# Third batch's q and k transposed by the DMA queue instead of TensorE: a threshold moved from 3 to 2

## The chip, the cores and the metric

The kernel runs on one core of one Trainium2 chip. The metric is device microseconds (us) of one launch, lower is better. Before the change three runs took 271.57, 271.71 and 272.1 us, a median of 271.71 us.

## The reference: what is computed

Inputs are q, k and v of shape (8 batches, 8 heads, 576 rows, 64 columns) and two weight matrices, w_in (512 x 2048) and w_out (2048 x 512), all float32. The output is 4608 x 512 float32. For each batch and head, a Nyström attention with 32 landmarks, and then one feed-forward layer over all heads' columns together:

```python
q_lm = q.reshape(B, H, m, S // m, D).mean(axis=3)     # m = 32 landmarks
k_lm = k.reshape(B, H, m, S // m, D).mean(axis=3)
A  = sm(q, k_lm)                                      # softmax of scaled scores
Bm = sm(q_lm, k_lm)
C  = sm(q_lm, k)
Z = Bm.T / (norm1(Bm) * norminf(Bm) + 1e-6)
for _ in range(6):
    Z = 2 * Z - Z @ Bm @ Z                            # inverse by Newton steps
x = A @ Z @ C @ v                                     # heads side by side: 4608 x 512
out = relu(x @ w_in) ** 2 @ w_out
```

## The kernel before, in words

**Stages.** The eight batches are numbered 0 to 7 here, so the "third batch" is batch 2. The kernel is a pipeline of stages, one for each batch b. In stage b, TensorE does the first product of the feed-forward layer for batch b (`mlp_in`, line 656: 16 pieces f of four matmuls), carries on with the second product for earlier batches (`mlp_out`, line 686), and between these does the attention of batch b+1. The attention is a Python generator, `attention(b + 1, R)`, that yields after each small piece. The main loop (lines 721 to 765) decides after which f how many pieces of it are issued: `steps` pieces in all (line 729), six tenths of them spread over the 16 pieces f, the rest over `mlp_out`. TensorE, VectorE and ScalarE then run in the order in which this weaving has put their instructions.

**The path of q and k.** For batch b, `load_qk` starts four transfers on GpSimd's DMA queue, which also convert float32 to bfloat16: the rows 512 to 575 of k and q into one small tile `qkt` (line 84), and the other 512 rows into `raw` tiles (line 96), two buffers shared by k and q. `prepare` copies a `raw` tile to `nat` on VectorE (line 188), which puts a head pair's columns side by side. The attention needs q and k both as they are (for the segment means, lines 253 and 263) and transposed, 128 x 128 block by block, as `T` (16 blocks each for q and k) and `tT` (four blocks from `qkt`). The transposed tiles are the stationary operands of the score matmuls (`scores`, line 408, and `tails`, line 418).

**Two ways to transpose.** Batches below `DMA_T` transpose on TensorE (lines 226 and 236) into PSUM, and VectorE or ScalarE copy the result to SBUF (lines 239, 548, 555, 558, 560). Batches from `DMA_T` on have it done by the DMA engines, issued from SP's queue: `tT` from line 196, `T` of k and of q from line 190, as soon as their source is there:

```python
            nc.vector.tensor_copy(X[nm][:], raw)
            if b >= DMA_T:
                nc.sync.dma_start_transpose(
                    X[nm + "T"].rearrange("p c a t -> p (c a) t"),
                    X[nm].rearrange("p c h d -> p (c h d)"))
```

**When `nat` is made.** The copies of line 188 are pinned behind a named instruction of the batch before (`kpin`, `qpin`). For batch 2 they are late: behind the copy to `WT` (line 609) and the last copy to `G` (line 642) of batch 1's attention, that is at the end of stage 0. For batch 3 and later they come behind the first joint step of the inverse of the batch before, which is in the middle of the stage ahead of the one that uses them.

**Weaving.** The same threshold sets `steps`: 28 where the attention in the stage transposes on TensorE, 24 where it does not. Of these 16 or 14 belong to the 16 pieces f. Within the attention the order is: segment means of k and of q, landmark scores and softmax, start of the inverse (lines 335 to 361), TensorE's transposes if any, and then pairs of an inverse step and a piece from `side`: scores of q (two halves), tails, scores of k (two halves), row sums, C times v.

**Queues.** GpSimd's DMA queue carries all loads from batch 1 on and both weight matrices, in program order; SP's queue carries batch 0's q and k, the DMA transposes and one of the last stores; ScalarE's queue carries the other stores.

Of the kernel before, what the change touches and what calls it, by code (L numbers as in the profile page):

```python
# [27 lines left out]
TAIL = S - NC4 * P  # L28
HALF = S // 2
SCALE = 1.0 / 8.0  # L30
DMA_T = 3


@with_exitstack
def kernel(
# [139 lines left out]
    def prepare(b: int, nms=("k", "q"), halves=((0, H),)):  # L175

        X = loaded[b]
        for nm in nms:
# [9 lines left out]
# [5 lines that stand above are left out]
        if "k" in nms:  # L193
            X["tT"] = attn.tile([P, NPAIR, P], BF16, tag="tT", name="tT")
            if b >= DMA_T:
                nc.sync.dma_start_transpose(X["tT"][:], X["qkt"].rearrange("p h d -> p (h d)"))
# [13 lines left out]
    def attention(b: int, R: dict):  # L210
# [6 lines left out]
        def transposed(nm, half):  # L217
            if not first:
                tps = ntile([P, 2, NPAIR, P], BF16)[:]
            else:  # L220
                if half == 0:
                    X["tps"] = psum.tile([P, 4, NPAIR, P], BF16, tag="h", bufs=2, name="tps")
                tps = X["tps"][:, 2 * half:2 * half + 2, :, :]
            for i in range(2):
                for p in range(NPAIR):
                    nc.tensor.transpose(
                        tps[:, i, p, :],
                        X[nm][:, 2 * half + i, 2 * p:2 * p + 2, :].rearrange("p h d -> p (h d)"),
                        ident_bf[:],
                    )  # L230
            return X[nm + "T"][:, 2 * half:2 * half + 2, :, :], tps
# [303 lines left out]
        else:  # L535
# [10 lines left out]
            yield  # L546
            if b < DMA_T:
                dve(*transposed("q", 0))
# [4 lines left out]
            yield  # L553
            if b < DMA_T:
                act(*transposed("q", 1))
# [165 lines left out]
    for b in range(B):  # L721
# [6 lines left out]
        att = attention(b + 1, R) if b + 1 < B else iter(())  # L728
        steps = 28 if b + 1 < DMA_T else 24
        half = steps * 6 // 10  # L730
# [67 lines left out]
```

The softmax here doesn't subtract the row's maximum and nothing guards it: scores larger than these inputs give would overflow.

## Time and profile before

One execution was profiled. Its own time was 271.57 us, with a span of 269.9 us from the first to the last instruction.

| what | value |
|---|---|
| median of three runs | 271.71 us |
| profiled execution: time, span | 271.57 us, 269.9 us |
| TensorE matmuls busy | 249.3 us (92% of the span) |
| VectorE busy, ScalarE busy | 176.2 us, 159.3 us |
| first `mlp_in` matmul of stages 1, 2, 3, 4 | 54.51, 84.71, 116.09, 144.37 us |
| DMA of loads (GpSimd's queue) | 17.17 MB |
| DMA of SP's queue (batch 0's q and k, transposes) | 8.39 MB |

Times are microseconds from the start of the span. An engine's busy time counts its data instructions; a matmul's end is modelled, since matmuls overlap. In a timeline, a row gives start, length, engine, line, operation, output and inputs, their shape, and how many instructions were merged; in brackets stands how long the engine stood idle before it, and what ended that. A name ending in q (SPq) is the engine's instruction queue, where DMAs are issued; the length of such a row is the time that issuing took, not that of the transfer. "DMA to landing" runs from the issue to the last byte's arrival.

### The profile page before, as it was taken

The page shows a single profiled execution, that of the slowest core. Times are in us where ns is not written, and L with a number is a line of the kernel's source. Part 1 is how long each engine was busy: PE and PEld are TensorE (multiplying, and loading weights), DVE is VectorE, ACT ScalarE, POOL GpSimd, SP SyncE. Part 2 cuts the span into 40 slices and gives each one's busy share as a digit, 9 for nine tenths or more (in the row PEclk, how much of TensorE's full clock was granted, in tenths as well). Part 3 has the DMA queues.
Part 4 walks back from the last instruction along what each step waited for, and adds up shares of the span by engine and source line. Part 5 has one row for each costly group of instructions (what it writes and reads, how often), then busy time and mean ns, then how long its engine had stood idle before and what let it go on. Part 6 is the DMA issues. An engine that isn't in the chain of part 4 may idle for free.

```text
span 269.9 us, 6741 instructions
## 1 busy us (share of the span) xinstructions
PE 249.3 (92%) x2747; PEld 149.6 (55%) x2793; DVE 176.2 (65%) x493; ACT 159.3 (59%) x280; POOL 43.4 (16%) x66
## 2 busy tenths in 40 slices
PE   2988799979999999999999999999999999999994
PEld 0754565457654665456555665466545665466444
DVE  4687878668884769458955779459954768545100
ACT  2478866448926766468726774568636674487111
POOL 3834333310320230220220231100000000000000
PEclk9999999999999999999999999999999999999999
DMA  7999999999699959993999969991911111200222
GB/s 206 244 205 196 205 204 187 229 188 134 82 157 196 167 119 152 179 155 53 141 166 149 143 121 154 144 163 39 198 41 39 41 39 41 78 34 9 78 78 80
DMA packets 69791, 35.31 MB, mean 131 GB/s; under 512 B 37376, under 2 KB 64256, under 8 KB 69760
## 3 DMA queue, kind: packets, MB, share of 16 engines
q0 software_dynamic: 37696, 17.17, 54.7%
q1 hardware_dynamic: 26816, 8.39, 21.8%
q10 hardware_dynamic: 5248, 9.31, 10.8%
q8 instruction: 22, 0.36, 0.6%
q14 instruction: 9, 0.07, 0.1%
HBM read 36.70 MB, written 9.44 MB: 171 GB/s over the span
## 4 chain that ended last, share of the span: by engine, by line
PE 62%; DMA 18%; ACT 7%; DVE 6%; issue 4%; POOL 1%; ACTq 0%; DVEq 0%; POOLq 0%
PE ops L686 31%; PE h L656 15%; DMA w_out_bf<-in_moe_w_out_dram 6%; PE n L686 6%; DMA raw<-in_q_dram 5%; DMA w_in_bf<-in_moe_w_in_dram 5%; ACT r L663 3%; ACT G L640 2%; PE g L627 2%; DMA raw<-in_k_dram 2%; DVE ra L432 2%; DVE gT L664 2%; PE n L454 1%; PE n L253 1%; PE n L408 1%
## 5 line engine op out<-in xcount | busy, mean ns | idle before, releaser
L686 PE MATMUL ops<-w_out_bf,gT 128*128 128x512 bf16 (+1 forms) x451 | 114.5, 371 | 3.2 <-DMA w_out_bf<-in_moe_w_out_dram 1.0
L663 ACT ACTIVATE r<-h 128x576 bf16<-128x576 f32 x128 | 82.9, 658 | 29.3 <-PE h L656 24.6
L656 PE MATMUL h<-AT,G 128*128 128x288 bf16 x512 | 83.3, 285 | 2.7 <-ACT G L640 1.0
L664 DVE TENSOR_TENSOR gT<-r 128x576 bf16<-128x576 bf16 x128 | 58.0, 454 | 32.7 <-ACT r L663 31.6
L686 PEld LDWEIGHTS <-gT 128*128 128x128 bf16 x592 | 53.4, 97 | 39.9 <-issue 6.9
L656 PEld LDWEIGHTS <-G 128*128 128x128 bf16 x512 | 45.4, 97 | 22.2 <-issue 5.7
L695 ACT COPY o_sb<-ops 128x512 f32<-128x512 f32 (+1 forms) x29 | 16.7, 578 | 35.2 <-PE ops L686 35.2
L686 PE MATMUL n<-w_out_bf,gT 128*128 128x512 bf16 x98 | 28.7, 380 | 0.4 <-issue 0.2
L642 DVE CAST G<-g 128x1024 bf16<-128x1024 f32 x14 | 17.1, 1224 | 12.7 <-PE g L627 12.7
L640 ACT CAST G<-g 128x1024 bf16<-128x1024 f32 x14 | 14.2, 1012 | 11.2 <-PE g L627 11.2
L408 PEld LDWEIGHTS <-T 128*128 128x128 bf16 x256 | 11.3, 98 | 5.4 <-issue 0.4
L325 PEld LDWEIGHTS <-ED 128*128 128x128 bf16 x84 | 7.2, 98 | 11.4 <-DVE ED L316 5.3
L444 DVE TENSOR_TENSOR an<-EA,rra 128x640 bf16<-128x640 f32 (+2 forms) x17 | 13.2, 779 | 0.2
L432 DVE TENSOR_REDUCE ra<-EA 128x20 f32<-128x640 f32 (+1 forms) x19 | 13.0, 701 | 0.4
L408 PE MATMUL n<-bd,T 128*128 128x64 bf16 x256 | 12.8, 193 | 0.1
L458 ACT COPY AT<-n 128x576 bf16<-128x576 bf16 x9 | 5.8, 639 | 11.8 <-PE n L454 11.8
L106 POOL DMA_DIRECT2D vm<-in_v_dram x8 | 7.0, 881 | 34.4 <-PE n L476 23.6
L253 PEld LDWEIGHTS <-nat 128*128 128x128 bf16 x256 | 9.0, 97 | 5.9 <-DVE nat L188 2.6
L96 POOL DMA_DIRECT2D raw<-in_k_dram x7 | 7.1, 1018 | 29.5 <-DVE nat L188 27.1
L84 POOL DMA_DIRECT2D qkt<-in_k_dram x7 | 5.1, 730 | 41.5 <-PE n L263 28.6
L188 DVE COPY nat<-raw 128x2048 bf16<-128x2048 bf16 x14 | 9.4, 688 | 2.5 <-DMA raw<-in_q_dram 1.8
L412 ACT ACTIVATE EA<-n 128x512 f32<-128x512 f32 x16 | 9.5, 601 | 2.0 <-PE n L408 2.0
(125 smaller groups left out, 267.1 us busy)
## 6 DMA issues: line engine op xcount, KB each, us to landing
out_dram<-o_sb ACTq DMA_DIRECT2D x31, 256.0 KB, 4.4
vm<-in_v_dram POOLq DMA_DIRECT2D x8, 512.0 KB, 14.0
raw<-in_k_dram POOLq DMA_DIRECT2D x7, 512.0 KB, 9.6
raw<-in_q_dram POOLq DMA_DIRECT2D x7, 512.0 KB, 13.5
w_in_bf<-in_moe_w_in_dram POOLq DMA_DIRECT2D x4, 512.0 KB, 10.6
w_out_bf<-in_moe_w_out_dram POOLq DMA_DIRECT2D x4, 512.0 KB, 16.2
out_dram<-o_sb ACTq DMA_DIRECT2D x9, 128.0 KB, 2.4
raw<-in_k_dram SPq DMA_DIRECT2D x1, 1024.0 KB, 5.6
```

The lines of the kernel that those rows point to most:

```text
L253: nc.tensor.matmul(means[:, ti, p, :], lhsT=src.rearrange("p h d -> p (h d)"), rhs=seg[:, c + (ti if c == NC4 else 0), :], start=(n == 0 a ...
L408: nc.tensor.matmul(sc[:, c, j, :, :], lhsT=X[nm + "T"][:, c, p, :], rhs=BD[:, 1 if nm == "q" else 0, p, 0:64], start=True, stop=True)
L412: nc.scalar.activation((EA if nm == "q" else EC)[:, qd, 0:NC4, :], sc.rearrange("p c j i m -> p c (j i m)"), AF.Exp, scale=SCALE)
L432: nc.vector.reduce_sum(ra[:, quads, lo:hi, :], EA[:, quads, lo:hi, :].rearrange("p q c (h m) -> p q c h m", m=M), axis=AX.X)
L444: nc.vector.tensor_tensor(an[:, i, lo:hi, :].rearrange("p c (h m) -> p c h m", m=M), EA[:, i, lo:hi, :].rearrange("p c (h m) -> p c h m", ...
L640: nc.scalar.copy(dst, gg[:])
L642: last = nc.vector.tensor_copy(dst, gg[:])
L656: last = nc.tensor.matmul(h[:, j, 0:HALF], lhsT=G[:, qd, f * P:(f + 1) * P], rhs=AT[:, qd, j * HALF:(j + 1) * HALF], start=(qd == 0), stop ...
L663: nc.scalar.activation(r.rearrange("p (j t) -> p j t", j=2), h[:, :, 0:HALF], AF.Relu)
L664: return nc.vector.tensor_tensor(gT[:, f, o:o + S], r[:], r[:], ALU.mult)
L686: mark[:] = [nc.tensor.matmul(ops, lhsT=gT[:, f, t * P:t * P + P], rhs=w_out_bf[:, f, i * n:i * n + n], start=(f == 0), stop=(f == NF - 1))]
L695: nc.scalar.copy(o_h, ops)
```

## The change

One constant:

```diff
-DMA_T = 3
+DMA_T = 2
```

It is read in five places: in `prepare` (lines 189 and 195), where batch 2 now gets the three DMA transposes on SP's queue; in `attention` (lines 547 and 554), where batch 2's TensorE transposes and their copies go away; and in the main loop (line 729), where stage 1, which holds batch 2's attention, goes from 28 steps to 24:

```python
            if b < DMA_T:
                dve(*transposed("q", 0))
            yield
            begun = inverse_begin()
            yield
            BT, ED = inverse_first(*begun)
            yield
            if b < DMA_T:
                act(*transposed("q", 1))
                ...
                transposed_tail()
```

Put together, the order of instructions on the queues changes as follows.

- SP's queue, from its sixth instruction on, held `tT` of batch 3, `T` of k and of q of batch 3, `tT` of batch 4 and so on. It now holds `tT` of batch 2, `tT` of batch 3, `T` of k and q of batch 2, `T` of k and q of batch 3, `tT` of batch 4 and so on.
- TensorE loses 36 transposes in stage 1. The score matmuls of batch 2's q, which stood behind f = 10, now stand behind f = 7, and their weight load waits for the DMA transpose of q.
- VectorE loses three copies and ScalarE two. Elsewhere in stage 1 their instructions change places in keeping with the steps.
- GpSimd's queue is the same.

## The prediction

> **What bounds the kernel now.** I read the page first: engine busy times, and the DMA row of the 40 slices (6.75 us each).
>
> ```profile
> PE 249.3 (92%) x2747; PEld 149.6 (55%) x2793; DVE 176.2 (65%) x493; ACT 159.3 (59%) x280; POOL 43.4 (16%) x66
> ...
> DMA  7999999999699959993999969991911111200222
> ```
>
> TensorE sets the pace, so time that it stands still is time lost. But the DMA engines are full for the first ten slices, up to about 67 us: loads run behind. So I read the timeline around the end of stage 0, where batch 2's q arrives:
>
> ```profile
> 51.81 0.69 DVE L188 COPY nat<-raw 128x2048 bf16<-128x2048 bf16 x1 [0.79 <-DMA raw<-in_k_dram]
> 55.40 0.69 DVE L188 COPY nat<-raw 128x2048 bf16<-128x2048 bf16 x1 [1.76 <-DMA raw<-in_q_dram]
> 56.43 1.29 SPq L196 DMA_TRANSPOSE tT<-qkt  x1
> 57.28 0.65 PE L656 MATMUL h<-AT,G 128*128 128x288 bf16 x4 [0.79 <-DVE G L642]
> 67.37 0.40 PE L408 MATMUL n<-bd,T 128*128 128x64 bf16 x8
> 70.39 11.90 SPq L190 DMA_TRANSPOSE T<-nat  x2
> 187.74 4.62 SPq L190 DMA_TRANSPOSE T<-nat  x2
> ```
>
> Batch 2's q is in `nat` only at 56.1 us; its first scores (line 408) run at 67.37 us, 11.3 us later, with TensorE's transposes between. SP's row at 56.43 is batch 3's `tT`, whose wait had ended on the load of `qkt` (the queue's wait list gives 51.3 us on it). 70.39 is batch 3's pair of `T`, 187.74 the last batch's.
>
> Then the transposing DMAs' own times (line 190, by window; lengths and landings as min/median/max, which for two is k's, the mean, q's): batch 3's pair, batch 4's, and batch 7's, when no load is left:
>
> ```profile
> L190 SPq DMA_TRANSPOSE T<-nat x2: 2023/5892/9762, 70.4 to 72.5; - x2
> DMA to landing us min/median/max: 11.2/15.8/20.3
> ...
> L190 SPq DMA_TRANSPOSE T<-nat x2: 3018/5123/7228, 97.6 to 100.7; - x2
> DMA to landing us min/median/max: 9.6/11.5/13.5
> ...
> L190 SPq DMA_TRANSPOSE T<-nat x2: 1741/2266/2791, 187.7 to 189.6; - x2
> DMA to landing us min/median/max: 4.4/6.0/7.7
> ```
>
> From k's issue to q's landing a pair takes 189.6 + 7.7 - 187.7 = 9.6 us with the engines free, 100.7 + 13.5 - 97.6 = 16.6 us and 72.5 + 20.3 - 70.4 = 22.4 us beside loads.
>
> **What the Trainium skill says.** *DMA: Bandwidth & Descriptors*, "Queues, rings and completion order": each DMA engine goes round between its queues packet by packet. The trace agrees: between 56 and 66 us the load queue moved 1.42 MB while batch 3's `tT`, 0.13 MB, took 7.2 us to land. The same page, "Latency and other measured facts", has 261 GB/s for a transposing DMA; here the free pair moved 1.05 MB in 9.6 us, 109 GB/s, and I use that. *TensorE: Matmul & The Clock Gate*, "Step-by-step: what each phase is for": matmuls stay in program order, only weight loads are pulled ahead; the 0.79 us wait at 57.28 us, with other batches' matmuls queued behind it, fits. The same page, "What's actually happening": after an idle window of about 3.4 us TensorE's clock halves, until some 3.4 us of work. The trace shows the like at the start, after 4.15 us of idling (granted clock 1.00 all the same): three 128x512 matmuls took 1.34 us at 9.78 us, and three of that shape take 0.82 us at 115.10 us.
>
> ```profile
> 7.13 1.89 PE L226 MATMUL tps<-ident_bf,nat 128*128 128x128 bf16 x16 [4.15 <-DVE nat L185]
> 9.78 1.34 PE L202 MATMUL idle<-bd 128*128 128x512 bf16 x3
> 115.10 0.82 PE L686 MATMUL n<-w_out_bf,gT 128*128 128x512 bf16 x3
> ```
>
> **The change part by part.**
>
> *Removed.* 32 transposes of line 226 and 4 of line 236. A group of eight spans 0.61 us, the last lasting 0.22, so one costs (0.61 - 0.22) / 7 = 0.056 us, and 36 cost 2.0 us of TensorE. With them go two ScalarE copies (1.01 and 1.05 us) and three on VectorE (0.69, 0.69, 0.42). TensorE was busy for 10.00 us of 57.3 to 67.4, so up to 2.0 us is a real gain, if nothing else stops it.
>
> *Added, SP's queue.* `tT` of batch 2 comes first. Its `qkt` is issued at 31.20 us and lands some 11 to 16 us later, so it runs in the full stretch: 0.13 MB at the 165 GB/s or so that the engines move beside transposes is 0.8 us, which every load behind it, and so q's arrival, loses. Next is `tT` of batch 3, which waits for its own `qkt` (56.43 us, now about 57.2) and takes 1.29 us to issue. Both `T` of batch 2 stand behind it: although k is in `nat` at 52.5 us, its transpose goes out at about 58.5 us, and q's after that. GpSimd's load of batch 4's `qkt`, which waited for TensorE's transposes (line 236) until 66.9 us, waits now for `tT` and the means of line 263, both done by about 59 us: 0.13 MB more beside the transposes.
>
> *How long the pair takes.* In the before trace the load queue still moves about 1.1 MB after 57.8 us (batch 3's q and k). Add 0.13 MB `qkt`, 1.18 MB transposes (pair and the `tT` ahead of it) and one store of 0.26 MB: 2.65 MB at 165 GB/s is 16 us. That is close to batch 4's 16.6 us. So q's transpose lands at 58.5 + 16 = 74.5 us. Bounds: 57.7 + 9.6 = 67.3 us with engines free and no shift; 58.5 + 22.4 = 80.9 us at batch 3's pace.
>
> *When it is wanted.* With 14 steps in place of 16 in the f pieces, and no transposes ahead, the scores of q stand behind f = 7. Before, f = 7 begins at 63.43 us with two groups of eight transposes ahead of it (60.10 and 62.99 us); without them, and with f = 7 itself (0.65 us) done, the new order reaches the scores at about 63 us. Their weight load waits for q's DMA. Behind it on TensorE stands everything: f = 8 to 15, the second product, the inverse. ScalarE and VectorE run dry within a microsecond or two and wait too. The stall is 74.5 - 63 = 11.5 us.
>
> *From there on.* Stage 3 is the model: also 24 steps, DMA transposes, the same five second-product tiles at its end. It runs from 116.09 to 144.37, with its first scores at 124.16 us, so 20.2 us pass from the scores to the next stage. Stage 2 therefore begins at 74.5 + 20.2 = 94.7 instead of 84.71 us: 10.0 us late, the removed work already counted in. Were q in time, it would begin at 63 + 0.8 + 20.2 = 84.0, 0.7 us earlier than now. The break-even landing is 84.7 - 20.2 = 64.5 us.
>
> *Cold clock.* An idle TensorE of over 3.4 us should come back at half clock for about 3.4 us, losing up to 1.7; ScalarE's relu (0.65 us a piece) hides a little. I take 1.5; bounds 0 and 3.4 (two windows).
>
> *Later stages.* Batch 3's pair goes out 3.9 us after the scores in stage 3's pattern (128.03 against 124.16), so at 78.4; at 22.4 us it lands at 100.8, and is wanted 9.5 us into stage 2, at about 104 or later. No second stall; the rest shifts unchanged.
>
> Sum against the profiled execution: 271.57 + 10.0 + 1.5 = 283.1 us. This execution lies 0.14 us below the median, nothing in these terms; I say 283.
>
> **Rivals.**
>
> *The pair runs almost free* (landing at 67.3 to 70.5): the transposes take the better share of the engines. For it: batch 4's k moved at 171 GB/s when the loads had not begun. Against: here the load queue is in full flow. 271.6 + 2.8 to 6, and a cold start of 0 to 1.5: 274.5 to 279, middle 277.
>
> *The pair starves* (landing after 78): batch 3's pair took 22.4 us with one load pair beside it. 271.6 + 13.5 to 16.4 + 1.5 = 286.5 to 289.5, middle 288.
>
> *The transfer is hidden* (faster): q's transpose lands by 64.5 us, TensorE never waits, and the removed 2.0 us show as far as the delayed loads let them: 271.6 - 0.7 = 270.9 us. It decides at a landing of 64.5 us. That needs the pair in about 7 us from 57.7, against 9.6 at best; only an SP order that lets k out at 52.5 could do it, and the instruction order says otherwise.
>
> *The change is empty in effect*, a stall that just eats the gain, takes the same 64.5 us landing within half a microsecond.
>
> **How the numbers follow.** Late by 71 to 78: 0.72; almost free: 0.15; starved: 0.08; hidden 0.03; even 0.02. The forecast is the likeliest, 283. The range, 276 to 288, corresponds to landings from about 68 (with the cold start) to 79, and leaves out the hidden and even cases and the outer part of the two others, under 2 in 10. A measurement here tells about 0.2% (0.5 us) from no change: faster 0.03, same 0.02, slower 0.95.
>
> **What will show it.** TensorE idle once, before the score matmuls of line 408 near 63 us, for 7 to 15 us, ended by the DMA of `T` from `nat`; on SP `tT` twice, the second near 57 us, and then four `T`; q's landing near 74.5; longer matmuls for some 3 us after; stage 2's first `mlp_in` at 95 to 96 us; later stages as long as before. I am wrong if q's transpose lands before 65 us, if TensorE has other matmuls to do in the wait, or if the stages after it win the time back.

## The result, and the profile after

| | before | after |
|---|---|---|
| median, us | 271.83 (4 runs, the three given above and 271.95) | 282.01 (4 runs, 281.0 to 283.71) |
| ratio after / before | | 1.0381, 95% interval 1.0329 to 1.0433 |
| profiled execution: time, span | 271.57, 269.9 | 282.07, 280.3 |

The change makes the kernel 10.2 us slower. The page of the kernel after, its engine and slice rows (7.0 us a slice):

```profile
PE 250.3 (89%) x2711; PEld 148.8 (53%) x2757; DVE 174.7 (62%) x490; ACT 157.7 (56%) x278; POOL 43.1 (15%) x66
...
PE   2888999872499999999999999999999999999995
...
PEclk9997999997599999999999999999999999999999
DMA  7999999999569994996199989991541010101222
```

TensorE's busy time went up by 1.0 us although it has 36 matmuls fewer, and its share fell from 92% to 89%: the work is there, there is a hole in it. The hole is in slices 9 and 10 (counted from 0), 63 to 77 us, and the granted clock is down in the same two. (The 7 in slice 3 is another, short dip of this execution, from 22.7 to 26.1 us, where the kernel is the same as before.)

The timeline around it, rows of VectorE, SP's queue and TensorE that answer to those shown of before:

```profile
53.40 0.69 DVE L188 COPY nat<-raw 128x2048 bf16<-128x2048 bf16 x1 [1.51 <-DMA raw<-in_k_dram]
56.95 0.70 DVE L188 COPY nat<-raw 128x2048 bf16<-128x2048 bf16 x1 [1.72 <-DMA raw<-in_q_dram]
...
46.11 13.24 SPq L196 DMA_TRANSPOSE tT<-qkt  x2
59.47 28.67 SPq L190 DMA_TRANSPOSE T<-nat  x4
...
64.28 0.65 PE L656 MATMUL h<-AT,G 128*128 128x288 bf16 x4
73.99 0.61 PE L408 MATMUL n<-bd,T 128*128 128x64 bf16 x8 [9.06 <-DMA T<-nat]
95.38 0.65 PE L656 MATMUL h<-AT,G 128*128 128x288 bf16 x4 [0.17 <-ACT G L640]
```

TensorE ends f = 7 at 64.9 us and then does nothing until q's transpose lands; the first matmul of stage 2 follows at 95.38 us, 10.7 us later than before. From there to the end pass 184.9 us, before 185.2: nothing is lost or won later. The transposes themselves (line 190 between 55 and 76 us; the second view is of the first of the pair alone):

```profile
L190 SPq DMA_TRANSPOSE T<-nat x2: 6114/6182/6251, 59.5 to 65.7; - x2
DMA to landing us min/median/max: 8.3/10.6/12.9
...
T<-nat SPq DMA_TRANSPOSE x1, 12.9
```

k's goes out at 59.47 and lands at 72.4; q's goes out at 65.69 and lands 8.3 us later, at 74.0. Last, the windows of TensorE, from the start of stage 1 to behind the hole (stretch, its length, TensorE's busy time and matmuls, granted clock, DMA share, GB/s; the DMA share adds up the times of packets, and passes 1 where packets of several queues are open at once):

```profile
57.00:65.00 8.00, 6.17 (x61) 1.00 1.48 190
65.00:74.00 9.00, 0.01 (x1) 0.62 1.30 173
74.00:77.40 3.40, 3.40 (x21) 0.51 0.02 5
77.40:84.00 6.60, 6.38 (x64) 1.00 0.72 110
```

While TensorE waits, the DMA engines are full; when it starts again, they are empty. For its first 3.3 us its clock is half, and from then on full again.

### The profile page after: what moved, and what is told of

Same layout as the page of the kernel before. It is cut to its first block, busy times and chain, and to the rows that moved or that the text cites. A ratio compares the mean times of both kernels' runs of the same rounds, so it can differ in the third digit from the quotient of the medians.

```text
span 280.3 us, 6675 instructions
## 1 busy us (share of the span) xinstructions
PE 250.3 (89%) x2711; PEld 148.8 (53%) x2757; DVE 174.7 (62%) x490; ACT 157.7 (56%) x278; POOL 43.1 (15%) x66
## 3 DMA queue, kind: packets, MB, share of 16 engines
q10 hardware_dynamic: 5248, 9.31, 10.2%
## 4 chain that ended last, share of the span: by engine, by line
PE 62%; DVE 11%; DMA 10%; ACT 10%; issue 5%; DVEq 0%; ACTq 0%
PE ops L686 29%; PE h L656 14%; DMA raw<-in_q_dram 5%; ACT r L663 5%; PE n L686 5%; DVE gT L664 3%; DMA T<-nat 3%; PE g L627 2%; ACT G L640 2%; DMA raw<-in_k_dram 2%; PE n L253 2%; DVE ra L432 2%; PE n L454 2%; PE n L325 1%; PE n L408 1%
## 5 line engine op out<-in xcount | busy, mean ns | idle before, releaser
L686 PEld LDWEIGHTS <-gT 128*128 128x128 bf16 x592 | 53.5, 98 | 40.6 <-issue 7.5
L640 ACT CAST G<-g 128x1024 bf16<-128x1024 f32 x14 | 14.2, 1012 | 11.1 <-PE g L627 11.1
L408 PEld LDWEIGHTS <-T 128*128 128x128 bf16 x256 | 11.6, 99 | 14.5 <-DMA T<-nat 9.4
L330 DVE SCALAR_TENSOR_TENSOR EY<-EY,n 128x128 bf16<-128x128 bf16 x24 | 6.8, 283 | 12.7 <-PE n L325 12.6
L325 PEld LDWEIGHTS <-ED 128*128 128x128 bf16 x84 | 7.4, 99 | 11.5 <-DVE ED L316 4.9
L627 PE MATMUL g<-w_in_bf,WT 64*32 64x512 bf16 x232 | 9.6, 389 | 2.0 <-DVE G L642 1.0
```

The lines of the kernel that those rows point to most:

```text
L325: nc.tensor.matmul(res[a:a + w, qd, :], lhsT=diagonal[a:a + w, qd, :], rhs=moving(qd)[a:a + w], start=True, stop=True)
L408: nc.tensor.matmul(sc[:, c, j, :, :], lhsT=X[nm + "T"][:, c, p, :], rhs=BD[:, 1 if nm == "q" else 0, p, 0:64], start=True, stop=True)
L627: nc.tensor.matmul(g[i][M * p:M * p + M, :], lhsT=WT[64 * i:64 * i + 64, i, M * p:M * p + M], rhs=w_in_bf[64 * i:64 * i + 64, p, n * 512:n ...
L640: nc.scalar.copy(dst, gg[:])
L686: mark[:] = [nc.tensor.matmul(ops, lhsT=gT[:, f, t * P:t * P + P], rhs=w_out_bf[:, f, i * n:i * n + n], start=(f == 0), stop=(f == NF - 1))]
```

## The experiments

Line numbers of an experiment's kernel can stand a few lines below those quoted so far (line 408, the score matmuls, is L409 or L414 in some).

**Nobody transposes batch 2.** Is the wait all that the change costs?

```diff
-                X[nm + "T"] = attn.tile([P, NC4, NPAIR, P], BF16, tag=nm + "T", name="T")
+                X[nm + "T"] = (loaded[1][nm + "T"] if b == 2 else attn.tile(...))
...
-            if b >= DMA_T:
+            if b > 2:
                 nc.sync.dma_start_transpose(
```

(and the same for `tT`)

> The changed kernel, but batch 2 is transposed by nobody: its scores read batch 1's transposed tiles, so batch 2's output is not the reference's. TensorE's instructions are those of the changed kernel in the same order. Theory (the late landing of q's transpose is the whole loss): no wait ahead of the score matmuls of line 408 in stage 1, and the 2.0 us of TensorE transposes are gained in part: 269.8 to 271.3 us, below the 271.8 of the kernel before. Rival (the new order of stage 1, 24 steps for 28, costs time by itself): 272.5 us or more, with idle time in stage 1 that is not ended by a DMA.

Measured: 270.62 us, ratio 0.9954 (0.9937 to 0.9971). TensorE's timeline:

```profile
63.49 0.40 PE L409 MATMUL n<-bd,T 128*128 128x64 bf16 x8
...
83.90 0.65 PE L657 MATMUL h<-AT,G 128*128 128x288 bf16 x4 [0.16 <-ACT G L641]
```

The scores run at 63.49 us, without a wait ahead of them, and stage 2 begins 0.8 us earlier than in the kernel before. So the new order and the missing transposes together win 1.2 us (0.8 to 1.7), of the 2.0 us that the 36 transposes take; what the order with 24 steps is worth by itself was not tried. Against this run the kernel after loses 11.4 us by the medians, and the profiles account for it: its scores come 10.5 us later (73.99 against 63.49), and from them to stage 2 pass 21.4 us, not 20.4.

**q's transpose ahead of k's.** Does TensorE wait for q's transpose or for the pair?

```diff
...
+            if b == 2 and nm == "q":
+                one = turn("q")
+                with tc.issue_after(one.ins):
+                    X["lastT"] = turn("k")
+            elif b > 2:
+                turn(nm)
```

> The changed kernel with batch 2's two big DMA transposes in the other order: q's first, k's behind it. Theory (TensorE waits for q's landing alone): q's goes out when k's did, at about 59.5 us, and lands 8.3 us later as k's did, at about 68; TensorE waits some 3 us in place of 9.1. k's lands at about 74, and its scores come some 7 us after q's, so they wait little or not at all. 275 to 277 us. Rival (the pair's whole time on the DMA engines decides, whichever is first): the wait moves to the scores of k, and the time stays at 280 to 282 us.

Measured: 279.94 us, ratio 1.0283 (1.0243 to 1.0322). SP's queue (two `tT` and four `T` in this window), the landing of the first transpose, now q's, and TensorE:

```profile
58.65 26.77 SPq L190 DMA_TRANSPOSE T<-nat  x4
...
T<-nat SPq DMA_TRANSPOSE x1, 12.7
...
71.44 0.61 PE L414 MATMUL n<-bd,T 128*128 128x64 bf16 x8 [7.34 <-DMA T<-nat]
```

Both expectations missed the time. The theory's 8.3 us for the first transpose was a misreading: in the changed kernel that is the landing of the second, and the first takes 12.9. q first takes 12.7 us; the wait falls from 9.1 to 7.3 us only, the time by 2.1 us, and k's scores don't wait, against the rival. Which is first matters little, because in either order both land when the loads are nearly through (at 72.4 and 74.0 us in the kernel after, 71.4 and 73.0 here).

**Dummy matmuls in the hole.** What does the clock cost?

```diff
+        if b == 2:
+            filler = ntile([P, 512])
...
+            with tc.issue_after(front[0].ins):
+                for _ in range(36):
+                    mm = nc.tensor.matmul(filler[:], lhsT=z[:, 0:P], rhs=z[:, 0:512], ...)
+            with tc.issue_after(mm.ins):
+                aside()
```

> The changed kernel with 36 dummy matmuls of 128x512 (some 7.8 us) on TensorE in the place where it stands still, ahead of batch 2's first scores. Theory (TensorE comes out of the wait at half clock and loses 1.2 us by it: 21.4 us from the scores to the next stage, against 20.2 in stage 3): the granted clock stays at 1.00 and the time is 280.8 us, 1.2 below the changed kernel. Rival (the clock after the wait costs nothing, the 1.2 us have another cause): 282 us, and still 21.4 us from the scores to the next stage.

Measured: 280.52 us, ratio 1.0305 (1.0268 to 1.0342). TensorE's timeline:

```profile
64.34 7.93 PE L578 MATMUL n<-bd 128*128 128x512 bf16 x36
73.84 0.41 PE L408 MATMUL n<-bd,T 128*128 128x64 bf16 x8 [1.57 <-DMA T<-nat]
93.64 0.65 PE L666 MATMUL h<-AT,G 128*128 128x288 bf16 x4 [0.17 <-ACT G L650]
```

The transpose lands at the same time (73.84 against 73.99 us), the granted clock is 1.000 over the whole run (0.976 in the changed kernel), and from the scores to stage 2 pass 19.8 us instead of 21.4. The medians of the two kernels lie 1.5 us apart; each was timed beside its own runs of the kernel before (271.86 and 271.83 us). The intervals of the two ratios just overlap, so the 21.4 and 19.8 us of the profiles carry the point as much as the medians. Work that computes nothing makes the kernel faster. Two pieces f behind the scores also stand in another order here, so of the 1.5 us a few tenths may belong to that.

**Batch 3's loads taken away.** Are the transposes slow because of what moves beside them?

```diff
-            for lo, hi in parts:
+            for lo, hi in ((0, 1),) if b == 3 else parts:
...
```

> The changed kernel with batch 3's loads of q and k cut to one head in eight (the head is spread to all eight places, so batch 3's output is not the reference's): some 0.9 MB less stands beside batch 2's DMA transposes. Theory (the transposes are slow because they share the engines with the loads that run behind): the pair takes about the 9.6 us that the last batch's takes, q's lands at about 69 us, TensorE waits some 4 us, 276 to 277.5 us. Rival (the transposes are held up by their own issue on SP's queue, k's then q's, whatever else moves): q's still goes out about 6 us after k's and lands at 73 to 74; 281 to 282 us.

Measured: 277.09 us, ratio 1.0170 (1.0126 to 1.0213). The two `T` of batch 2 and TensorE:

```profile
L191 SPq DMA_TRANSPOSE T<-nat x2: 2990/3036/3082, 58.5 to 61.6; - x2
DMA to landing us min/median/max: 5.4/5.8/6.1
...
67.78 0.61 PE L409 MATMUL n<-bd,T 128*128 128x64 bf16 x8 [3.05 <-DMA T<-nat]
```

The pair goes out 1.0 us earlier than in the kernel after, is issued twice as fast (3.0 us each, not 6.2), and takes 61.6 + 6.1 - 58.5 = 9.2 us, not 14.5. This is the theory's case. Even so the kernel is slower than before: with most of the loads gone the transposes still come 3 us late. The profile is of the quickest of four runs (275.73 us, clock 0.994); the other three took 277.0 to 277.4 at 0.980. Their longer time at half clock fits that; they have no profile.

**Batch 3's small transpose behind.** Is it the place on SP's queue?

```diff
...
+                with tc.issue_after(loaded[2]["lastT"].ins) if b == 3 else nullcontext():
                     nc.sync.dma_start_transpose(X["tT"][:], ...)
```

> The changed kernel with batch 3's small DMA transpose put behind both big ones of batch 2 on SP's queue, in place of ahead of them; k's then goes out as soon as k is copied, at about 54, not 59.5 us. Theory (the engines' share decides: the transposes move only as the load queue lets them): they start moving some 4 us earlier, but the same bytes stand in front, and q, copied at about 57 us, is second; q's lands at 70 to 72 us, 279 to 281 us. Rival (the wait behind the small transpose on SP's queue is what makes them late): q's lands 5 us earlier, at 68 to 69 us, 275 to 277 us.

Measured: 282.64 us, ratio 1.0401 (1.0379 to 1.0424). SP's queue, the first transpose's landing, TensorE:

```profile
53.52 13.58 SPq L190 DMA_TRANSPOSE T<-nat  x2
...
T<-nat SPq DMA_TRANSPOSE x1, 12.9
...
73.64 0.61 PE L409 MATMUL n<-bd,T 128*128 128x64 bf16 x8 [9.54 <-DMA T<-nat]
```

k's goes out 6 us earlier and lands 6 us earlier, at 66.4 us. q's goes out 7.2 us earlier (58.5, not 65.7) and lands at 73.6 us all the same. So the queue in front of the transposes held k's, but not q's, the last of the pair. Moving earlier, they take from the loads: batch 3's k and q land 12.6 and 13.9 us after their issue, not 9.3 and 10.0. The theory had the kind right, but its 70 to 72 us for the landing, and its time with it, were too low.

**Batch 2's v behind its q and k**, on the kernel after (expected first below) and on the kernel before (second). Is it the late q?

```diff
...
-            load_v(b + 2, loaded[b + 2])
+            with tc.issue_after(loaded[2]["lastraw"].ins) if b == 0 else nullcontext():
+                load_v(b + 2, loaded[b + 2])
```

> The changed kernel with the same move: batch 2's v loaded behind its q and k. Theory (a transpose beside the full load queue gets a third of the engines, so that q's lands only when the loads have drained, whenever it was issued; the move leaves the bytes as they are): q and k are copied some 3 us earlier, their transposes still land at 71 to 74 us, TensorE reaches the scores earlier and waits longer, 280 to 282 us. Rival (it is the late arrival of q that makes its transpose late): q's lands 3 us earlier, at about 70 to 71 us, and the time falls by 3 to 278.5 us or below.

> The kernel before, with batch 2's loads of v (0.6 MB) put behind its q and k on GpSimd's queue, in place of ahead of them; nothing else changes place. Theory (the loads that run behind are the root: batch 2's q arrives late for TensorE even in the kernel before): q lands some 3 us earlier, at 52 to 53 us, the 1.6 us that TensorE stood idle around 55 us go, and v is wanted only at about 77 us: 270.0 to 270.8 us. Rival (the waits around 55 us are the chain's, not the load's; v comes late for the products with C): 271.6 us or more.

Measured: on the kernel after 281.47 us, ratio to the kernel before 1.0355 (1.0339 to 1.0372). VectorE and TensorE:

```profile
53.33 0.68 DVE L188 COPY nat<-raw 128x2048 bf16<-128x2048 bf16 x1
...
72.95 0.61 PE L408 MATMUL n<-bd,T 128*128 128x64 bf16 x8 [11.04 <-DMA T<-nat]
```

q is copied 3.6 us earlier, its transpose lands 1.0 us earlier, and TensorE, which is at the scores sooner, waits longer: 11.0 us. The late q alone is thus not it; but the transposes went out only 0.9 and 0.6 us earlier (58.6 and 65.1 us), since batch 3's `tT` still stood in front of them. The two experiments were not put together. With v moved, `tT` behind and q first, q's could go out at 54.0 us; as the first of a pair landed 12.5 to 14.2 us after its issue wherever batch 2's moved beside full loads, it would land at about 67 us, by estimate. TensorE, at the scores from 61.9 us on, would still wait some 5 us; the change would lose less, but still lose.

On the kernel before: 269.28 us, ratio 0.9913 (0.9900 to 0.9926). Its copies, and the start of stage 2:

```profile
50.79 0.68 DVE L188 COPY nat<-raw 128x2048 bf16<-128x2048 bf16 x1
52.83 0.68 DVE L188 COPY nat<-raw 128x2048 bf16<-128x2048 bf16 x1
...
82.39 0.65 PE L656 MATMUL h<-AT,G 128*128 128x288 bf16 x4 [0.17 <-ACT G L640]
```

Neither copy waits for its load any more, and stage 2 begins 2.3 us earlier. The gain is larger than the theory's (270.0 us at best). This version beats both kernels: 2.5 us below the kernel before, by the order of loads alone. It shows that the late loads cost time in the kernel before, too, and were worth moving; transposing with the DMA engines goes the other way.

**k alone by DMA.** q, wanted first, stays on TensorE; here on the kernel before and, second, together with the move of v.

```diff
-            if b >= DMA_T:
+            if b >= DMA_T or (b == 2 and nm == "k"):
...
-                if b > 1:
-                    dve(*transposed("k", 0))
-                    yield
-                    act(*transposed("k", 1))
-                    yield
...
-        steps = 28 if b + 1 < DMA_T else 24
+        steps = 28 if b == 0 else 26 if b == 1 else 24
```

> The kernel before, with batch 2's k alone transposed by the DMA engines (26 steps in stage 1): q, which is wanted first, and the small tile stay on TensorE. k's DMA transpose goes out as soon as k is in its bf16 tile, at about 52.5 us, ahead of batch 3's small one on SP's queue. Theory (a DMA transpose costs nothing where it lands before its first use): it lands when the load queue drains, at 66 to 70 us, and its first score matmuls stand at about 72 us, so TensorE doesn't wait; 16 transposes (0.9 us) leave TensorE, and the time is 270.7 to 271.7 us, at best 0.4% below the kernel before. Rival (the 0.5 MB beside the loads delays batch 2's q or batch 3's loads, which are needed just then): 272.5 to 274 us, with idle time ended by a DMA of raw.

> Batch 2's k alone by DMA transposes (q and the small tile on TensorE), with batch 2's v loaded behind its q and k. Theory (k's transpose is hidden, and the move of v gives its gain independently): the same as the move alone on the kernel before, or up to 0.5 us below it, 269.6 to 270.8 us. Rival (k's transpose, now moving while q and v of batch 2 and q and k of batch 3 load, lands late or makes batch 3's loads late): over the move alone by 0.5 us or more.

Measured: alone 271.51 us, ratio 0.9994 (0.9984 to 1.0003), no difference. With the move of v 273.25 us, ratio 1.0050 (1.0027 to 1.0072), that is 4 us above the move alone. VectorE and TensorE of the second, ahead of them VectorE's copies in the move alone:

```profile
67.24 1.28 DVE L188 COPY nat<-raw 128x2048 bf16<-128x2048 bf16 x2
...
67.49 0.69 DVE L188 COPY nat<-raw 128x2048 bf16<-128x2048 bf16 x1 [1.79 <-DMA raw<-in_k_dram]
70.63 0.69 DVE L188 COPY nat<-raw 128x2048 bf16<-128x2048 bf16 x1 [1.88 <-DMA raw<-in_q_dram]
...
68.81 0.23 PE L325 MATMUL n<-EY,ED 128*128 128x64 bf16 x2 [1.35 <-DVE ED L316]
72.52 0.23 PE L325 MATMUL n<-EY,ED 128*128 128x64 bf16 x2 [1.84 <-DVE ED L316]
```

k's transpose (out at 51.7, landing at 64.9 us) is never waited for. But batch 3's q and k, which load beside it, come late for their copies, which in the move alone ran at 67.24 us without a wait; VectorE stands at each copy for 1.8 us, with the inverse of batch 2 queued behind, and TensorE waits for that. The transfer is hidden, and what it takes from its neighbours is not. This was the rival.

**Independent work in front of the wait.** The scores are held back until all 16 pieces f are issued.

```diff
-            attend(early[f] if b == 0 else (f + 1) * half // NF)
+            attend(early[f] if b == 0 else min((f + 1) * half // NF, 6 if b == 1 else half))
...
         tiles = mlp_out(b, gT)
+        half = 6 if b == 1 else half
```

> The changed kernel with batch 2's score matmuls held back until all 16 first-product pieces of stage 1 are issued (six attention pieces in front of them, the other 18 behind), so that some 7 us of independent TensorE work stand where TensorE waited 9.1 us. Theory (the wait costs only because everything independent is queued behind it): the wait at line 408 shrinks to 3 us or less, the clock stays up, and part of the gain is given back where the rest of the inverse has less work beside it: 274.5 to 278 us. Rival (the chain of the inverse, which can't begin its joint steps until the scores are out of the way, sets stage 1's end): 281 us or more, with TensorE idle behind the scores instead of ahead of them.

Measured: 277.35 us, ratio 1.0198 (1.0163 to 1.0233). TensorE:

```profile
69.12 1.14 PE L656 MATMUL h<-AT,G 128*128 128x288 bf16 x8
75.62 0.56 PE L408 MATMUL n<-bd,T 128*128 128x64 bf16 x7 [5.36 <-DMA T<-nat]
```

The wait is 5.4 us, not the 3 at most that were expected: the eight pieces f covered some 6 us, and q's transpose landed 1.6 us later than in the kernel after. One more store of 256 KB had been issued into the transfer (at 70.04 us), and between k's issue and q's landing the engines moved 2.96 MB, not 2.60; that may be why, and was not tried apart. Nor did the clock stay up here: it was half from 73.0 to 79.9 us. This is the slowest of four runs (278.19 us, clock 0.981; the others 275.1 to 277.5, clock 0.994). The time came out within the theory's range.

## Why the prediction was right

- **The sum.** Forecast 283 us, measured 282.0; the range, 276 to 288, and the sign hold. In the profiled execution stage 2 is late by 10.7 us (forecast 10.0 + 1.5), and TensorE waits for 9.06 us. The sum came out closer than its parts, which is luck in part.
- **The landing** (74.5 forecast, 74.0 measured). Two errors cancel in it: k's transpose went out 1.0 us later than forecast (59.5, not 58.5), and the pair took 14.5 us, not 16. The bytes were right (2.65 MB forecast, 2.60 MB moved in these 14.5 us), the rate was 179 GB/s, not 165. The step, bytes in front over the rate of full engines, is the one that the runs support: with 1.78 to 3.63 MB between the first issue and q's landing, the rate was 170 to 193 GB/s in all six kernels where q's is the last of the pair. q's lands at 73.6 us where it goes out 7 us earlier, at 75.6 with one more store beside it, at 71.4 as the first, and at 67.8 when 0.9 MB of loads are taken away.
- **When it is wanted** was mis-sized: about 63 us forecast, 64.9 measured. 0.8 us for the delay of the loads by batch 2's `tT` was in another term, not in this one. Of the other 1.1 us, 0.7 were there early: in this execution GpSimd's queue was behind before `tT` ever ran (29.50 against 28.76 us at batch 2's `qkt`). The transfer of batch 2's q, 13.5 us before and 14.3 after, fits the 0.8 us that `tT` was priced at, but does not show it: in the five other kernels with `tT` on the queue and the same loads ahead of it, the copy of q began anywhere from 55.95 to 56.74 us. So the stall was 9.1, not 11.5 us; since the end follows from the landing, this did not enter the sum.
- **The removed work** was said to be worth 0.7 us if q came in time. Without `tT`'s 0.8 us of delay the same working gives 1.5 us; with nobody transposing it was 1.2 us, by the medians.
- **The cold clock** (1.5 forecast): 21.4 us from the scores to stage 2 against 20.4 with no wait, and 1.5 us between the medians with and without dummy matmuls. The granted clock shows it in the view itself: 0.62 in the hole and 0.51 in the 3.4 us after. That it came back after 3.3 us is chance: in the five other profiles with a wait of 3 us or more it took 3.2 to 5.5 us (the last section has the stretches at half clock), so it could have cost more, though not beyond the 3.4 us given as the bound.
- **The rivals.** *Almost free* happened only when most of batch 3's loads were gone (9.2 us for the pair, 9.6 forecast with engines free). *Starved* and *hidden* did not happen. One sentence of the hidden rival was wrong: an SP order that lets k out early did not do it. That order was run, and q landed at 73.6 us. The 171 GB/s given for batch 4's k is about its 0.52 MB over the 3.0 us of its issue; from issue to landing it took 9.6 us, 55 GB/s.
- **Later stages.** Batch 3's pair went out at 78.2 us and landed at 97.6 (78.4 and 100.8 forecast), and no matmul waited for it.

## What to carry to other kernels

Handing work from a busy engine to the DMA engines needs these to be free, and time as well: here the pair took 9.2 us even with most loads gone, and came 3 us late. Under full load, the landing of the last of several transfers followed from the bytes still to be moved and the engines' rate, and issuing it 7 us earlier changed nothing; the landing of the first followed its issue, at the cost of the loads beside it. Ask of each transfer what it will take from its neighbours too: one that nobody waits for can still cost time by making a load late. Where an in-order engine idles at a stage's start for a load, try the order of the loads first; here that won 2.5 us, where the change lost 10.2.

## What the runs showed of the hardware

- Beside a full load queue, DMA transposes got about a third of the bytes. The DMA queues between 62 and 66 us in the kernel after (q0 carries the loads, q1 SP's transposes):

```profile
q0 software_dynamic: 1064, 0.50, 93.0%
q1 hardware_dynamic: 932, 0.23, 44.4%
```

- That is 58 GB/s for the transposes and 125 GB/s for the loads. With the loads through, between 72 and 74 us, the transposes moved 0.39 MB in 2 us, 195 GB/s. From first issue to last landing a pair with few loads or none beside it moved 1.05 MB in 9.2 to 9.6 us, 109 to 114 GB/s.
- The two queues took turns by packets, not by bytes: 532 of loads and 534 of transposes between 64 and 66 us, 673 and 677 between 66 and 68 us; with batch 3's small transpose behind, 481 and 480 between 62 and 64 us. The third of the bytes comes from the sizes, about 250 bytes a packet for the transposes and 470 for the loads between 62 and 66 us. Loads in small packets take as many turns for less: the 673 packets were 0.12 MB.
- Issued at 53.5 or at 59.5 us, the first of a pair took the same 12.9 us to land.
- The issue of a DMA transpose on SP's queue took 6.1 and 6.3 us beside loads in the kernel after (4.8 to 8.6 us in the other experiments that transpose both), and 3.0 us each with most of the loads gone. In the run with the small transpose behind, q's went out 7.2 us earlier and landed no earlier, so for q's the slow issue was a sign of full engines and not the cause of the delay.
- TensorE's granted clock fell to 0.50 in steps of about 3.4 us. It was half from 67.1 to 77.3 us in the kernel after, 66.0 to 76.2 with q first, 67.6 to 71.0 with light loads, 68.9 to 79.2 with the small transpose behind, 66.6 to 76.8 with v behind, and 73.0 to 79.9 with the scores held back: one, two or three times 3.4 us. The dip from 22.7 to 26.1 us is one such step too, and the longest wait of TensorE between 18 and 23 us was 0.66 us. This agrees with the Trainium skill, *TensorE: Matmul & The Clock Gate*, "What's actually happening", on the window's length and on its running freely. It differs on the condition, a whole idle window: with q first the clock fell 1.9 us into the wait, with the small transpose behind 4.8 us into it.
